# Another order of steps in a kernel of beacon attention and a multiplicative feed-forward layer

## The chip, the cores and the metric

The kernel runs on one core of a Trainium2 chip. The metric is the device time of one launch in microseconds (us), the median of three runs. The profile is of one execution; its span begins with the first instruction of the program, and all times of day in the text are microseconds from that start. TensorE is called PE in the profile, VectorE DVE, ScalarE ACT, GpSimd POOL and SyncE SP.

## The reference

Eight batches with eight heads of 576 positions and 64 elements go through causal attention, in which 16 beacon keys and values stand ahead of the sequence and are seen by all. The result, 4608 tokens of 512 elements, goes through a feed-forward layer that multiplies two projections.

```python
B, H, S, Nb, D = (8, 8, 576, 16, 64)
k_all = np.concatenate([beacon_k, k], axis=2)
v_all = np.concatenate([beacon_v, v], axis=2)
scores = scale * np.matmul(q, k_all.transpose(0, 1, 3, 2))
causal[:, Nb:] = np.triu(np.ones((S, S), dtype=bool), k=1)
scores = np.where(causal, -1000000000.0, scores)
scores = scores - scores.max(-1, keepdims=True)
a = np.exp(scores)
a /= a.sum(-1, keepdims=True) + 1e-09
attn = np.matmul(a, v_all)
# ... transposed to x: (4608, 512)
a = x @ w1            # (512, 1024)
b = x @ w2            # (512, 1024)
h = a * b @ w3        # (1024, 1024)
out = h @ w_out       # (1024, 512)
```

Inputs and output are float32. The kernel computes in float16 with float32 sums.

## The kernel before

The kernel is a set of small steps and a list, `ORDER`, that names them one after another. The list is the program: it is walked once, and each step adds its instructions to the queues of the engines that it uses, in that order. Within an engine the order is kept; between engines semaphores hold back whatever needs something that is not done. The last number of many steps is a bank of PSUM, a letter A or D says whether ScalarE or VectorE copies, and P or S whether GpSimd or SyncE issues a store.

```python
ORDER = """
consts 0; consts 1; consts 2; spin 8 7; lq 0 0 S; lkb 0; lk 0 1 S; lk 0 0 S; lq 0 1 S; lvb 0; lo 0;
lo 1; cast 0 0 q; castb A; l3 0; tq 0 0 6; tn 0 7; cast 0 1 k; l3 1; eq 0 0 A 6; en 0 D 7; l3 2;
tk 0 1 5; cast 0 0 k; l3 5; ek 0 1 A 5; spin 1 7; tk 0 0 6; lo 2; ek 0 0 A 6; lo 3; spin 3 7;
s 0 0 0; s 0 1 2; s 0 2 4; exp 0 0 0; cast 0 1 q; spin 1 7; tq 0 1 6; exp 0 1 2; m 0 0 0; l3 3;
eq 0 1 D 6; exp 0 2 4; m 0 0 1; spin 3 7; s 0 3 0; s 0 4 2; lv 0 1; exp 0 3 0; spin 1 7; s 0 5 4;
# ... 117 lines ...
o 8 0 7; eo 8 1 A 6; st 8 1 S; eo 8 0 A 7; st 8 0 S; o 8 3 6 0 256; eo 8 3 A 6 0 256;
st 8 3 S 0 256; o 8 3 5 256 256; eo 8 3 A 5 256 256; st 8 3 S 256 256
"""
```

The product of w3 and w_out is formed once, as `Wt`, so that a token needs one matrix in place of two. For that each block `r` of w3 (128 rows) is loaded and cast (`l3`), transposed by TensorE (`t3`), copied to SBUF (`e3`) and multiplied with w_out (`f`, four parts; part `a` needs quarter `lo a`), and the result is copied (`ew`). Transposed blocks lie in four places of `gTs[1]`, and block `HELD` in the first 128 columns of the last four store buffers `st8`.

```python
    HELD = 2
    # ...
    def wT(r):

        if r == HELD:
            rows = st8[:, ds(4, 4), 0:P].bitcast(FP16)
        else:
            rows = gTs[1][:, ds(2 * slot["wT", r], 2), :].rearrange("p a (b n) -> p (a b) n", b=2)
        return rows.rearrange("p a (r c) -> p a r c", c=P)

    def l3(r):
        nc.gpsimd.dma_start(w316[:, r // 2, r % 2], moe_w3[ts(r, P), :])

    def lo(a):
        nc.gpsimd.dma_start(wo16[:, ds(2 * a, 2), :], wo_v[a])

    def t3(r, n):
        pt = bank16(n).rearrange("p (r c) -> p r c", c=P)
        for rt in range(NFT):
            nc.tensor.transpose(pt[:, rt, :], w316[:, r // 2, r % 2, ts(rt, P)], ident)

    def f(r, a, n):
        for rt in (2 * a, 2 * a + 1):
            nc.tensor.matmul(
                bank(n),
                wT(r)[:, a, rt % 2, :],
                wo16[:, rt, :],
                start=(rt == 0),
                stop=(rt == NFT - 1),
            )
```

For batch 0, q and k of a pair of heads come in whole through SyncE, in float32, into the buffers `st8` (eight places, in the order of loading; a load into one of the last four waits until `f HELD` has read its part there). VectorE casts them (`cast`) and TensorE transposes them (`tq`, `tk`), ScalarE or VectorE copy them to `qTs` and `kTs` (`eq`, `ek`). For later batches GpSimd's queue loads and casts rows of all heads, and they are transposed either by TensorE (`tq`, `tk`) or by a transfer on SyncE (`Dq`, `Dk`).

```python
    def lq(b, c, e, src=q, z="q"):
        if b == 0:
            nc.sync.dma_start(
                sts[take("own", (z, c), NOWN)][:NR].rearrange("p (h n) -> p h n", h=2),
                src[b, ds(2 * c, 2)].rearrange("h (p j) d -> p h (j d)", j=RUN),
            )
        elif z == "q":
            load_rows(b, c, q, by_heads(q16s[b % NB2]))
        else:
            load_keys(b, c, k, by_heads(k16s[b % NB2]))

    def cast(b, t, z):
        o16 = o16s[z][take("o16" + z, t, 2)]
        nc.vector.tensor_copy(
            o16[:NR].rearrange("p j (h d) -> p h j d", h=2),
            sts[slot["own", (z, t)]][:NR].rearrange("p (h j d) -> p h j d", h=2, j=RUN),
        )

    def tq(b, c, n, z="q"):
        if b == 0:
            o16 = o16s[z][slot["o16" + z, c]]
            for j in range(RUN):
                nc.tensor.transpose(
                    bank16(n)[:, ds(j * NR, NR)], o16[:NR, j, :], ident[:NR, :NR]
                )
            return
        w = rows_of(z, c)
        for t in range(NT):
            nc.tensor.transpose(
                bank16(n)[:, ds(t * P, w)],
                (q16s, k16s)[z == "k"][b % NB2][:w, c, ts(t, P)],
                ident[:w, :w],
            )

    def Dq(b, c):
        rows = rows_of("q", c)
        nc.sync.dma_start_transpose(
            qTs[b % NB2][:, :, ds(c * P, rows)], q16s[b % NB2][:rows, c, :]
        )
```

Scores come in 13 groups for each batch (`s b g bank`), each is exponentiated (`exp`), masked on the diagonal (`m`), multiplied with v (`v`) and divided by its sum (`n`), and the result is transposed by TensorE (`x`, `ex`) or by a transfer (`TX`). The feed-forward layer runs on 512 tokens at a time: `a` and `b` are the two projections, `ea` copies the first, `eb` multiplies, `o` is the product with `Wt`, `eo` the copy and `st` the store.

```python
    def a(mc, kf, n, i=0):
        for kt in range(NKT):
            nc.tensor.matmul(
                bank(n),
                w12[:, kt, ds(i * DF + kf * P, P)],
                xT[:, kt, ds(mc * 512, 512)],
                start=(kt == 0),
                stop=(kt == NKT - 1),
            )

    def o(mc, mt, n, c0=0, w=DM):
        for kf in range(NFT):
            nc.tensor.matmul(
                bank(n)[:, 0:w],
                gTs[mc % 2][:, kf, ts(mt, P)],
                Wt[:, kf, ds(c0, w)],
                start=(kf == 0),
                stop=(kf == NFT - 1),
            )

    def spin(reps, n):
        for _ in range(reps):
            nc.tensor.matmul(bank(n), zeros[:, 0:P], zeros)

    def consts(part):
        if part == 0:
            nc.vector.memset(zeros, 0.0)
            nc.vector.memset(ident, 1.0)
            nc.vector.memset(MX, 1.0)
            nc.vector.memset(MD, 1.0)
            for i in range(NB2):
                nc.vector.memset(kTs[i][:, :, ds(S + Nb, NJT * P - S - Nb)], 0.0)
            nc.vector.memset(ring[:, :, :, GW:GP], 0.0)
            for i in range(NB2):
                nc.vector.memset(vas[i][64:128, 4, :, :], 0.0)
                nc.vector.memset(vas[i][:, 0:4, :, D : D + 1], 1.0)
                nc.vector.memset(vas[i][0 : S + Nb - 4 * P, 4, :, D : D + 1], 1.0)
        elif part == 1:
            nc.gpsimd.affine_select(
                ident,
                ident,
                pattern=[[1, P]],
                compare_op=ALU.is_equal,
                fill=0.0,
                base=0,
                channel_multiplier=-1,
            )
        elif part == 2:
            for msk, base in ((MX[:, 0:112], Nb), (MX[:, 112:192], 0), (MD, 0)):
                nc.gpsimd.affine_select(
                    msk,
                    msk,
                    pattern=[[1, msk.shape[1]]],
                    compare_op=ALU.is_ge,
                    fill=0.0,
                    base=base,
                    channel_multiplier=-1,
                )
```

`spin` multiplies zeros and its result isn't used: it keeps TensorE busy while it has nothing else to do. `consts 1` and `consts 2` make the identity and the two masks; they run on GpSimd, the engine that also issues the casting transfers.

Of the kernel before, what the change touches and what calls it, by code (L numbers as in the profile page):

```python
# [74 lines left out]
f 4 1 5; lq 1 1 P; tq 0 3 6; f 4 2 5; exp 0 7 2; eq 0 3 D 6; v 0 0 1 7; l2 1; m 0 2 0; v 0 0 0 6;
n 0 0 1 7; v 0 2 0 4; s 0 8 0; s 0 9 2; l1 0; n 0 2 0 4; exp 0 8 0; v 0 1 1 7; n 0 0 0 6; f 4 3 5;
lq 1 4 P; n 0 1 1 7; exp 0 9 2; t3 6 6; lk 1 1 P; tk 1 4 4; ew 4 D 5; s 0 10 0; e3 6 A 6;
v 0 1 0 7; ek 1 4 D 4; s 0 11 2; s 0 12 4; lkb 1; n 0 1 0 7; exp 0 10 0; f 6 0 6; m 0 2 1; l2 2;
tq 1 0 7; f 6 1 6; m 0 3 0; exp 0 11 2; eq 1 0 D 7; f 6 2 6; v 0 2 1 7; lv 1 3; exp 0 12 4;
m 0 3 1; t3 7 3; n 0 2 1 7; lq 1 2 P; v 0 3 0 2; e3 7 A 3; v 0 3 1 5; n 0 3 0 2; tq 1 1 7; f 6 3 6;  # L80
l1 2; n 0 3 1 5; eq 1 1 A 7; x 0 0 4; x 0 4 3; ew 6 A 6; f 7 0 2; ex 0 0 D 4; x 0 2 7; ex 0 4 D 3;
x 0 1 6; lq 1 3 P; ex 0 2 A 7; x 0 3 5; ex 0 1 D 6; tq 1 4 4; f 7 1 2; ex 0 3 A 5; eq 1 4 D 4;
lk 1 0 P; f 7 2 2; tk 1 1 6; a 0 1 7; l2 0; ek 1 1 A 6; l1 3; f 7 3 2; ea 0 1 A 7; b 0 4 6;
ew 7 D 2; lk 1 2 P; a 0 0 7; lk 1 3 P; tq 1 2 5; ea 0 0 A 7; b 0 2 4; lk 2 0 P; eq 1 2 D 5;
a 0 2 7; lv 1 2; a 0 4 5; lv 1 0; ea 0 2 A 7; eb 0 2 4; tq 1 3 7; lv 1 1; tk 1 0 3; eq 1 3 A 7;
a 0 5 2; ek 1 0 D 3; b 0 0 7; lk 2 2 P; b 0 1 4; eb 0 0 7; lvb 1; a 0 6 3; eb 0 1 4; lq 2 2 P;
tk 1 2 7; ea 0 4 A 5; ea 0 5 D 2; a 0 3 4; lkb 2; ek 1 2 A 7; ea 0 6 D 3; tk 1 3 5; lq 2 3 P;
b 0 5 7; eb 0 4 6; ek 1 3 A 5; ea 0 3 D 4; lk 2 1 P; s 1 0 0; s 1 1 2; s 1 2 4; eb 0 5 7;
# [593 lines left out]
```

## Time and profile before

| | |
|---|---|
| time, median of three runs | 296.28 us (295.73 to 296.83) |
| span of the profiled execution | 295.1 us |
| busy: TensorE, ScalarE, VectorE, GpSimd | 286.5, 162.8, 156.1, 133.1 us |
| first scores of batch 0 (L492) start | 10.0 us |
| first transposes of w3 (L468) start | 15.2 us |
| bytes moved by the casting queue (GpSimd) and by the plain queue (SyncE) | 26.86 MB and 12.25 MB |

A page of the profile has busy shares, a picture of the span in 40 slices of 7.4 us with a digit for tenths of busy time, the chain of work that ended last (followed back from the end, at each step to what released it), groups of instructions by line of the kernel, and transfers. A line such as `PE one L564 x48` means 48 matmuls of line 564 into a PSUM tile named `one`. Busy times of matmuls overlap each other, since the next starts before the one before it has drained. In a list of waits the columns are: engine and what waited, what it waited for, microseconds in all, how often, and the longest. In a timeline they are the start, the length, the engine, the line and the operation. L345 are the plain loads of q and k of batch 0, L387 those of w_out, L384 of w3, L468 the transposes of w3, L477 the product with w_out, L406 the transposes of q and k of batch 0, L492 scores, L605 warm-up.

### The profile page before, as it was taken

What the parts mean: (1) busy time and instruction counts of PE and PEld (TensorE: products, weight loads), DVE (VectorE), ACT (ScalarE), POOL (GpSimd) and SP (SyncE); (2) the same over time, 40 slices, a digit from 0 to 9 for tenths busy, and PEclk for the clock granted to TensorE, in tenths of its full rate; (3) what the DMA queues carried; (4) which work ended last, traced back from release to release, by engine and by line L of the source; (5) the groups of instructions that cost most, each with busy time, mean ns of one, the idle gap of its engine ahead of it and who ended that gap; (6) DMA issues with size and microseconds to landing.
All of it is one profiled execution on the core that took longest, in us unless ns stands there. A gap on an engine that the chain in (4) does not pass through costs nothing.

```text
span 295.1 us, 7052 instructions
## 1 busy us (share of the span) xinstructions
PE 286.5 (97%) x2914; PEld 156.9 (53%) x2914; DVE 156.1 (53%) x350; ACT 162.8 (55%) x211; POOL 133.1 (45%) x185
## 2 busy tenths in 40 slices
PE   6997999999999999999999999999999999999995
PEld 2454675466665655655545554555456444544443
DVE  5323772786677756765427565466667262430430
ACT  3654794488784975748337542763377233443232
POOL 8464787979866384682288710662001000201000
PEclk9999999999999999999999999999999999999999
DMA  7999999999999999999999992899933110331004
GB/s 169 209 190 252 188 173 171 141 143 129 174 166 144 166 140 187 118 132 155 180 204 162 150 252 25 92 132 168 117 87 97 27 38 0 115 83 71 36 32 149
DMA packets 153617, 39.56 MB, mean 134 GB/s; under 512 B 143217, under 2 KB 150129, under 8 KB 153585
## 3 DMA queue, kind: packets, MB, share of 16 engines
q0 software_dynamic: 114320, 26.86, 99.6%
q1 hardware_dynamic: 39264, 12.25, 28.5%
q8 instruction: 23, 0.38, 0.5%
q14 instruction: 10, 0.07, 0.1%
HBM read 39.32 MB, written 9.44 MB: 165 GB/s over the span
## 4 chain that ended last, share of the span: by engine, by line
PE 83%; DMA 11%; ACT 2%; DVE 1%; issue 1%; POOL 1%; SPq 0%; DVEq 0%; POOLq 0%
PE one L564 38%; PE one L585 20%; PE one L523 9%; PE pair L492 8%; DMA k<-in_k_dram 4%; DMA st<-in_k_dram 4%; DMA kT<-k 3%; PE one L477 3%; ACT ring L502 2%; PE one L605 2%; PE one L412 1%; PE one L549 1%; PE one L468 1%; PE one L406 1%; DVE o16k L394 0%
## 5 line engine op out<-in xcount | busy, mean ns | idle before, releaser
L564 PE MATMUL one<-xT,w 128*128 128x512 f16 x576 | 133.2, 379 | 0.0
L502 ACT ACTIVATE ring<-pair 128x1024 f16<-128x1024 f32 x104 | 99.0, 1027 | 16.0 <-PE pair L492 15.6
L564 PEld LDWEIGHTS <-w 128*128 128x128 f16 x576 | 53.4, 98 | 59.8 <-issue 1.7
L579 DVE TENSOR_TENSOR gT<-one,asb 128x512 f16<-128x512 f32 x72 | 49.1, 689 | 56.9 <-PE one L564 32.9
L585 PE MATMUL one<-Wt,gT 128*128 128x512 f16 (+1 forms) x296 | 66.8, 373 | 0.0
L300 ACT ACTIVATE asb<-one 128x512 f32<-128x512 f32 x52 | 31.0, 597 | 64.9 <-PE one L564 34.1
L599 POOL DMA_DIRECT2D out_dram<-st x32 | 18.1, 565 | 94.3 <-ACT st L300 59.7
L334 POOL DMA_DIRECT2D va<-in_v_dram x40 | 34.0, 857 | 35.4 <-PE one L523 29.9
L585 PEld LDWEIGHTS <-gT 128*128 128x128 f16 x296 | 27.6, 98 | 30.2 <-issue 0.8
L523 PEld LDWEIGHTS <-ring 128*128 128x128 f16 x960 | 34.7, 98 | 9.4 <-issue 1.2
L523 PE MATMUL one<-va,ring 128*128 128x65 f16 x960 | 37.6, 193 | 0.0
L326 POOL DMA_DIRECT2D q<-in_q_dram x35 | 29.9, 856 | 6.2 <-PE one L412 1.7
L535 DVE TENSOR_TENSOR x<-one,rd 128x256 f16<-128x256 f32 (+1 forms) x64 | 31.4, 491 | 2.2
L492 PE MATMUL pair<-qT,kT 64*128 64x80 f16 (+4 forms) x736 | 31.2, 228 | 0.6 <-DMA kT<-k 0.4
L334 POOL DMA_DIRECT2D k<-in_k_dram x35 | 29.7, 854 | 3.3 <-DMA va<-in_v_dram 1.6
L300 ACT ACTIVATE st<-one 128x512 f32<-128x512 f32 (+1 forms) x24 | 13.9, 579 | 31.2 <-PE one L585 31.2
L492 PEld LDWEIGHTS <-kT 64*128 64x128 f16 x736 | 20.7, 96 | 14.1 <-issue 9.1
L512 DVE TENSOR_TENSOR ring<-ring,MD 128x768 f16<-128x768 f16 x32 | 17.7, 552 | 11.4 <-ACT ring L502 11.4
L302 DVE TENSOR_SCALAR asb<-one 128x512 f32<-128x512 f32 x20 | 13.6, 688 | 8.8 <-PE one L564 8.7
L534 DVE RECIPROCAL rd<-one 128x4 f32<-128x4 f32 (+1 forms) x64 | 11.8, 184 | 10.8 <-PE one L523 10.3
L512 DVE TENSOR_TENSOR ring<-ring,MX 128x384 f16<-128x384 f16 x32 | 11.3, 352 | 9.3 <-ACT ring L502 9.3
L477 PE MATMUL one<-wo,gT 128*128 128x512 f16 x56 | 14.8, 380 | 0.4 <-DVE gT L296 0.4
(56 smaller groups left out, 132.5 us busy)
## 6 DMA issues: line engine op xcount, KB each, us to landing
out_dram<-st POOLq DMA_DIRECT2D x32, 256.0 KB, 5.6
q<-in_q_dram POOLq DMA_DIRECT2D x28, 128.0 KB, 6.6
va<-in_v_dram POOLq DMA_DIRECT2D x24, 128.0 KB, 7.6
k<-in_k_dram POOLq DMA_DIRECT2D x21, 128.0 KB, 7.0
xT<-in_moe_w_dram POOLq DMA_DIRECT2D x8, 256.0 KB, 9.8
w<-in_moe_w_dram POOLq DMA_DIRECT2D x8, 256.0 KB, 7.6
st<-in_q_dram SPq DMA_DIRECT2D x4, 288.0 KB, 7.1
st<-in_k_dram SPq DMA_DIRECT2D x4, 288.0 KB, 5.7
```

Of the source, the lines that this page charges most:

```text
L300: nc.scalar.activation(dst, src, AF.Copy, scale=by)
L326: nc.gpsimd.dma_start(dst[:rows, c], src[b, :, ds(c * P, rows), :].rearrange("h s d -> s h d"))
L334: nc.gpsimd.dma_start(dst[ds(p0, rows), c], src[b, :, ds(s0, rows), :].rearrange("h s d -> s h d"))
L477: nc.tensor.matmul(bank(n), wT(r)[:, a, rt % 2, :], wo16[:, rt, :], start=(rt == 0), stop=(rt == NFT - 1),)
L492: nc.tensor.matmul(shape(n, "pair")[:, hh, ds(col, w)], kT[ds(hh * 64, 64), t, ts(jt, P)], qT[ds(hh * 64, 64), t, ds(q0, w)],)
L502: nc.scalar.activation(held(b, g)[:, :, 0:GW], shape(n, "pair"), AF.Exp, scale=scale)
L512: nc.vector.tensor_tensor(blk, blk, msk, ALU.mult)
L523: nc.tensor.matmul(pv[:, 2 * at + hh, 0 : D + 1], held(b, g)[:, hh, ds(col, P)], va[:, jt, 2 * t + hh, 0 : D + 1], start=(jt == 0), stop=( ...
L535: nc.vector.tensor_tensor(x16s[b % NB2][:, ds(2 * h, ni), ts(t, P)].rearrange("p i (h d) -> p i h d", h=2), pv[:, 0 : 2 * ni, 0:D].rearran ...
L564: nc.tensor.matmul(bank(n), w12[:, kt, ds(i * DF + kf * P, P)], xT[:, kt, ds(mc * 512, 512)], start=(kt == 0), stop=(kt == NKT - 1),)
L579: nc.vector.tensor_tensor(gTs[mc % 2][:, kf, :], bank(n), asb[slot["asb", (mc, kf)]], ALU.mult)
L585: nc.tensor.matmul(bank(n)[:, 0:w], gTs[mc % 2][:, kf, ts(mt, P)], Wt[:, kf, ds(c0, w)], start=(kf == 0), stop=(kf == NFT - 1),)
```

## The change

Only `ORDER` changes. All steps, buffers and sizes stay as they are. The list was computed anew, so nearly every line differs; what differs in kind is this:

- GpSimd issues the first quarter of w_out (`lo 0`) ahead of the identity, and the masks (`consts 2`) only behind three quarters of w_out and four blocks of w3. Before, all constants stood first.
- The first loads on SyncE are k, q of the second pair, beacon k, q, k of the second pair; before they were q, beacon k, k of the second pair, k, q of the second pair.
- Blocks 0, 2, 1 and 3 of w3 come first, before 0, 1, 2 and 5. Block 2 is the one held in the store buffers in both. Block 0 is transposed behind three groups of scores, before behind six.
- The last four loads of q and k of batch 0 are q, q, k, k; before k, k, q, q.
- There are 16 warm-up matmuls in five places; before 22 in nine.
- The tile with the last output is the third of its 512 tokens; before the fourth. It is computed in two halves in both.
- One tile of q more is transposed by TensorE (15 in place of 14), and 24 transfers `Dq` are left of 25. Of `x` and `TX`, `Dk` and `tk` the numbers stay, with other tiles.
- VectorE copies six of the eight transposed blocks of w3, before three; ScalarE 57 of the 72 first projections, before 52.

It is meant to have the weights at hand sooner, so that TensorE finds work on `Wt` while the second pair of heads is still on its way, with fewer warm-ups.

```diff
 ORDER = """
-consts 0; consts 1; consts 2; spin 8 7; lq 0 0 S; lkb 0; lk 0 1 S; lk 0 0 S; lq 0 1 S; lvb 0; lo 0;
-lo 1; cast 0 0 q; castb A; l3 0; tq 0 0 6; tn 0 7; cast 0 1 k; l3 1; eq 0 0 A 6; en 0 D 7; l3 2;
-tk 0 1 5; cast 0 0 k; l3 5; ek 0 1 A 5; spin 1 7; tk 0 0 6; lo 2; ek 0 0 A 6; lo 3; spin 3 7;
-s 0 0 0; s 0 1 2; s 0 2 4; exp 0 0 0; cast 0 1 q; spin 1 7; tq 0 1 6; exp 0 1 2; m 0 0 0; l3 3;
-eq 0 1 D 6; exp 0 2 4; m 0 0 1; spin 3 7; s 0 3 0; s 0 4 2; lv 0 1; exp 0 3 0; spin 1 7; s 0 5 4;
-spin 2 7; t3 0 6; l3 4; exp 0 5 4; m 0 1 0; e3 0 D 6; exp 0 4 2; spin 2 7; t3 1 7; lv 0 4; m 0 1 1;
-f 0 0 6; e3 1 D 7; f 0 1 6; lv 0 0; t3 2 5; f 1 0 7; e3 2 A 5; f 1 1 7; lv 0 3; t3 5 4; f 2 0 5;
-e3 5 A 4; f 2 1 5; lk 0 2 S; lv 0 2; f 2 2 5; lk 0 3 S; f 5 0 4; lq 0 2 S; f 1 2 7; f 2 3 5; l1 1;
-f 0 2 6; ew 2 A 5; lq 0 3 S; f 0 3 6; f 5 1 4; ew 0 A 6; l3 6; t3 3 5; f 5 2 4; e3 3 A 5;
-cast 0 2 k; f 5 3 4; f 1 3 7; lk 1 4 P; ew 5 D 4; tk 0 2 6; ew 1 A 7; f 3 0 5; ek 0 2 D 6; f 3 1 5;
-f 3 2 5; cast 0 3 k; f 3 3 5; tk 0 3 6; l2 3; ew 3 A 5; cast 0 2 q; t3 4 7; ek 0 3 A 6; tq 0 2 4;
-e3 4 D 7; lq 1 0 P; eq 0 2 A 4; spin 1 5; f 4 0 5; cast 0 3 q; s 0 6 0; s 0 7 2; l3 7; exp 0 6 0;
-f 4 1 5; lq 1 1 P; tq 0 3 6; f 4 2 5; exp 0 7 2; eq 0 3 D 6; v 0 0 1 7; l2 1; m 0 2 0; v 0 0 0 6;
# ... 106 lines ...
-a 8 5 4; eb 8 3 5; b 8 6 3; ea 8 5 A 4; eb 8 5 6; a 8 6 5; b 8 7 6; a 8 4 4; eb 8 7 6; a 8 0 2;
-ea 8 6 A 5; ea 8 4 D 4; b 8 4 6; eb 8 6 3; ea 8 0 A 2; eb 8 0 7; b 8 1 5; eb 8 4 6; a 8 1 7;
-o 7 1 6; ea 8 1 A 7; eb 8 1 5; o 8 2 7; eo 7 1 A 6; st 7 1 P; o 8 1 6; eo 8 2 A 7; st 8 2 S;
-o 8 0 7; eo 8 1 A 6; st 8 1 S; eo 8 0 A 7; st 8 0 S; o 8 3 6 0 256; eo 8 3 A 6 0 256;
-st 8 3 S 0 256; o 8 3 5 256 256; eo 8 3 A 5 256 256; st 8 3 S 256 256
+consts 0; lk 0 0 S; lq 0 1 S; lo 0; consts 1; spin 8 7; lkb 0; lo 1; lq 0 0 S; lk 0 1 S; l3 0;
+l3 2; l3 1; cast 0 0 k; l3 3; tk 0 0 6; lo 3; consts 2; cast 0 1 q; ek 0 0 A 6; lo 2; castb D;
+spin 2 7; tq 0 1 7; tn 0 6; eq 0 1 A 7; en 0 D 6; cast 0 0 q; l3 4; tq 0 0 5; eq 0 0 A 5;
+cast 0 1 k; spin 3 7; s 0 0 0; s 0 1 2; s 0 2 4; exp 0 0 0; lv 0 2; tk 0 1 6; ek 0 1 D 6;
+exp 0 1 2; spin 2 7; t3 0 7; l3 5; m 0 0 0; s 0 3 0; s 0 4 2; e3 0 D 7; exp 0 2 4; t3 2 6; lv 0 1;
+m 0 0 1; f 0 0 7; exp 0 3 0; e3 2 D 6; f 0 1 7; lvb 0; t3 1 5; exp 0 4 2; m 0 1 0; f 2 0 6;
+e3 1 D 5; f 2 1 6; lq 0 3 S; lv 0 4; s 0 5 0; lq 0 2 S; t3 3 5; exp 0 5 0; f 1 0 4; e3 3 D 5;
+lv 0 0; f 1 1 4; m 0 1 1; f 3 0 3; f 3 1 3; spin 1 5; f 0 2 7; lv 0 3; f 2 2 6; f 2 3 6;
+cast 0 3 q; lk 0 2 S; f 3 2 3; ew 2 A 6; lk 0 3 S; f 3 3 3; f 1 2 4; ew 3 A 3; lq 1 3 P;
+cast 0 2 q; t3 4 6; f 1 3 4; e3 4 A 6; l3 7; tq 0 2 5; ew 1 D 4; tq 0 3 3; f 0 3 7; eq 0 2 A 5;
+eq 0 3 D 3; f 4 0 6; ew 0 A 7; f 4 1 6; cast 0 2 k; f 4 2 6; l1 0; tk 0 2 7; t3 5 5; ek 0 2 A 7;
+f 4 3 6; e3 5 D 5; lk 1 2 P; s 0 6 0; s 0 7 2; ew 4 A 6; cast 0 3 k; f 5 0 7; exp 0 7 2; lkb 1;
+f 5 1 7; l3 6; tk 0 3 6; exp 0 6 0; f 5 2 7; l2 3; ek 0 3 D 6; f 5 3 7; v 0 0 0 5; l1 3; m 0 2 0;
# ... 105 lines ...
+a 8 0 4; ea 8 3 A 6; eb 8 3 7; b 8 7 6; ea 8 0 A 4; eb 8 0 5; b 7 3 7; eb 8 7 6; b 7 6 5; b 7 0 6;
+a 7 3 4; a 7 6 2; ea 7 3 A 4; eb 7 3 7; a 8 5 4; ea 7 6 A 2; eb 7 6 5; a 7 0 7; ea 8 5 A 4;
+eb 8 5 3; o 8 3 5; ea 7 0 A 7; eb 7 0 6; o 7 3 6; eo 8 3 A 5; st 8 3 S; o 7 0 7; eo 7 3 A 6;
+st 7 3 P; o 8 1 6; eo 7 0 A 7; st 7 0 P; o 8 0 7; eo 8 1 A 6; st 8 1 S; o 7 2 6; eo 8 0 A 7;
+st 8 0 S; o 7 1 7; eo 7 2 A 6; st 7 2 P; eo 7 1 A 7; st 7 1 S; o 8 2 6 0 256; eo 8 2 A 6 0 256;
+st 8 2 S 0 256; o 8 2 5 256 256; eo 8 2 A 5 256 256; st 8 2 S 256 256
 """
```

## The prediction

> **What bounds the kernel now.** I read the page first: its share of busy time, its slices, and the chain that ended last; then the chain in order of time, the list of waits for TensorE, and the timelines of the two engines that issue transfers.
>
> ```profile
> PE 286.5 (97%) x2914; PEld 156.9 (53%) x2914; DVE 156.1 (53%) x350; ACT 162.8 (55%) x211; POOL 133.1 (45%) x185
> ...
> PE   6997999999999999999999999999999999999995
> ...
> DMA  7999999999999999999999992899933110331004
> ```
>
> TensorE is busy in 97% of the span and the next engine in 55%. Only slices 1, 4 and the last are thin (a slice is 7.4 us). DMA is full until slice 24 of 40, so TensorE can't run far ahead of the loads either.
>
> ```profile
> 1.75 4.58 DMA st<-in_k_dram
> ...
> 8.77 1.28 PE one L605 x3
> ...
> 19.89 6.25 DMA st<-in_k_dram
> ...
> 173.59 10.36 PE one L564 x48
> ...
> 193.10 11.56 DMA k<-in_k_dram
> 204.68 9.85 DMA kT<-k
> 214.82 1.83 PE one L585 x8
> ...
> 283.42 8.67 PE one L585 x48
> ```
>
> This is the chain (start, length, what). In the middle, 48 matmuls of 512 columns take 10.36 us, 0.216 us each, with nothing between them. At 8.77 us three warm-up matmuls of the same size take 1.28 us, 0.427 each: TensorE is at half speed there. So time is lost in the first 30 us and in the tail, while the middle is matmuls at their rate. What TensorE waited for says the same:
>
> ```profile
> PE one L406 <- DVE o16k L394: 3.2, 2, 1.9
> PE one L605 <- DVE zeros L609: 1.3, 1, 1.3
> PE pair L492 <- DMA kT<-k: 0.4, 2, 0.3
> PE one L477 <- DVE gT L296: 0.4, 1, 0.4
> ```
>
> Only 5.3 us of waiting are named in 295. The largest, 3.2 us, are the casts of k of the first batch, which wait for their loads. These two timelines show how the loads start:
>
> ```profile
> 0.81 0.40 SPq L345 DMA_DIRECT2D st<-in_q_dram  x1
> 1.27 0.43 SPq L359 DMA_DIRECT2D bst<-in_beacon_k_dram  x1
> 1.75 0.92 SPq L345 DMA_DIRECT2D st<-in_k_dram  x2
> 2.71 0.45 SPq L345 DMA_DIRECT2D st<-in_q_dram  x1
> 19.89 0.81 SPq L345 DMA_DIRECT2D st<-in_k_dram  x2
> ```
>
> ```profile
> 2.35 0.71 POOL L370 DMA_DIRECT2D va<-in_beacon_v_dram  x1
> 3.06 1.46 POOL L387 DMA_DIRECT2D wo<-in_moe_w_out_dram  x2
> 4.48 2.19 POOL L384 DMA_DIRECT2D xT<-in_moe_w_dram  x4
> ```
>
> The first four loads of q and k go out on SyncE from 0.81 us. GpSimd, whose queue casts the weights, starts at 2.35 us, behind its constants. The packet records show the plain queue alone until about 4.5 us at 230 GB/s, and the first weight packets only at 6.7 us, when that queue has nearly drained.
>
> **What the Trainium skill says.** "Perfetto Trace Analysis", section "Identifying the Most-Contended Engine", warns that busy time of matmuls does not measure distance from the limit. The trace agrees: a matmul of 512 columns is listed with 379 ns on the page, but they start 0.216 us apart. I therefore count starts, not busy time. "TensorE: Matmul & The Clock Gate", section "Part 1: The HAM clock gate (the "warmup" mystery)", says that the clock is halved until TensorE has been busy through one window of about 3.4 us, and that the window runs freely. The trace agrees on the two rates (0.427 and 0.216 us); the full rate is there from 13.3 us. "DMA: Bandwidth & Descriptors", section "Issuing engines are not separate DMA queues", says that transfers issued by any engine run on the same 16 DMA engines and interleave. From 24 to 28 us the trace agrees: about 65 packets of each queue in each half microsecond. At 4.5 to 6.5 us it agrees less: the later starter got about half as many packets as the other.
>
> **The change part by part.** Only the list of steps changes; all loop bodies, buffers and the arithmetic stay.
>
> Work removed from TensorE: the warm-up matmuls go from 22 to 16 (8+1+3+1+3+1+2+2+1 before, 8+2+3+2+1 after). At 0.216 us that is 6 x 0.216 = 1.3 us; at half speed up to twice that. Transposes: 14 tiles of q go through TensorE before and 15 after, which adds 4 x 0.056 = 0.2 us (eight of L468 take 0.45 us in the chain). Net -1.1 us. The matmuls of the projections, scores and values keep their number, and the last tile of the output is in halves in both lists. Adding every step at its measured spacing gives 271.1 us before and 270.1 after.
>
> Work that moves: I added up this work ahead of the same step in both lists, and compared it with the times in the trace. The seventh group of scores of the first batch stands behind 19.8 us of work and starts at 31.1, so 11.3 us have been lost by then. The first scores of the second batch stand behind 44.6 and start at 56.8 (12.2 lost), of the eighth behind 194.8 at 213.7 (18.9 lost); all of it is 271.1, done at 292 (20.8 lost). From the second batch on the loss grows evenly, about 0.09 us with each of the 91 remaining groups of scores, 8.2 of 8.6 us. It comes with the groups, and stays. What the change can move is the 12 us at the front, small stalls later, and the 3 us tail.
>
> The front, after the change: GpSimd issues the first half-megabyte of w_out at about 0.9 us instead of 3.06, and k, q, beacon k, q, k follow on SyncE. The first packets of that queue came 2.2 us after its first issue (2.35 to 4.5), so now they should come at 3.1 us, when about 190 of the 768 packets of q and k have gone. If the two queues share packet for packet, at about 170 packets a microsecond together, the third big load (q of the first heads, which the first scores need) lands at 8.6 us and the fourth at 10.9, against 7.5 and 8.7 before. Then cast 0.7, six transposes 0.65, copy 0.65 and the warm-up: first scores at 11.2 us, 1.2 later than the 9.98 of before. If the plain queue keeps its precedence, as it had at 4.5 to 6.5 us, they start at about 9.7.
>
> What is gained back: the first block of w3 is transposed right behind three groups of scores and one tile of k, not behind six groups and two warm-ups. Its data are there at about 12.1 us in both. So the transposes start at 12.6 to 14.0 us instead of 15.18. All w3 work moves about 1 to 2 us ahead, and with it the point at which the four loads of the second heads may overwrite the held block. Before, those were issued at 19.89 us, and TensorE stood still for 1.9 us at 24.9 for the first of them. After, the two q go first, at about 17, and k at about 20; I expect a stall of about 1 us at the transposes of q. Loss at the seventh group of scores: 10 to 11 us instead of 11.3.
>
> Later: each load's end in the queue of before (by adding up packets), laid under the new order, shows less room. The tightest load stands 6.7 us of work behind its use for batch 2 in the old order and 7.9 in the new; for the batch 3 tile now transposed by TensorE it is 8.9. With 1.2 us for completion, the new order needs a front loss of at least 10 us to run without waits. So whatever the front gains beyond 1 to 2 us, these waits take back. For batch 8 the same two links of the chain (11.56 and 9.85 us) remain: SyncE issues 12 transposes one behind another, 1.2 to 2 us apart, between the last scores of batch 6 and the first of batch 8; the room is 26.8 us of work against 28.4 before, but one transpose fewer. I count a wait of 0 to 1 us there, as now (0.8).
>
> Sum: -1.1 (work), +1.2 to -1 (front, mid +0.1), +0.7 (less room in the middle, an allowance and not a count), tail 0. Together -0.3 us: 296.28 becomes 296.0.
>
> **The rivals.** First, the early weights crowd out q and k. For it: packets alternate at 24 to 28 us. Against: at 4.5 to 6.5 us the first queue kept its rate. If it is worse than one to one, the first scores come at 12 to 13 us, TensorE has gaps in the window in which it should warm up, and half speed lasts one window (3.4 us) longer, which costs 1.7 us more: 298 to 300.
>
> Second, the transfers become the bound in the middle. For it: DMA is full through slice 24 and the room shrinks by 1 to 3 us for batches 2 to 4; an order made from estimated durations can be wrong in 90 places. Against: the old order comes from the same kind of estimate and shows only 0.8 us of waits behind 31 us. This would make it 297 to 299.
>
> Third, the front gains fully: transposes of w3 at 12.6, no stall for the second heads, and the middle has more room than I count. For it: 2.3 us of the old waits lie exactly there. Then it loses 9.5 us at the front, and the time is 293.5 to 294.5.
>
> **Range and chances.** The work is fixed to 1 us, and the tail is the same; only about 12 us at the front and a few small stalls can move. I take 296.0 us, from 293.4 (third rival) to 299.5 (first) as the range. Two per cent are 5.9 us, half of all that the front loses, so faster by that much has 3%, slower 5% (both bad rivals at once), within 92%.
>
> **What would show it.** In the changed profile: 16 matmuls of L605; the first w_out issue at about 0.9 us and its packets near 3.1; the first scores (L492) at 9.7 to 11.2; the first transposes of L468 at 12.6 to 14.0; waits of L406 for the casts of about 1 us at 23 to 27; the seventh group of scores near 28 to 29; the eighth batch's at 208 to 210 with a wait for kT of at most 1 us; the last matmul near 291. It is wrong if the clock warms up at a different time by a whole window, or if waits for loads of more than 2 us appear between 40 and 110 us.

## The result, and the profile after

| | before | after |
|---|---|---|
| time, median | 296.04 us (295.73 to 296.83, four runs) | 299.19 us (298.85 to 300.02, four runs) |
| ratio to before, 95% interval | 1 | 1.0106 (1.0076 to 1.0137) |
| span of the profiled execution | 295.1 us | 297.3 us |
| first scores of batch 0 | 10.0 us | 12.4 us |
| first transposes of w3 | 15.2 us | 15.0 us |
| first product with w_out (L477) | 16.6 us | 16.6 us |
| seventh group of scores of batch 0 | 31.1 us | 32.5 us |
| first scores of the second batch | 56.8 us | 57.1 us |
| last matmul starts | 291.8 us | 294.0 us |

The change makes the kernel 3.15 us slower, 1.1%. That is less than the 2% that counts as slower here, and inside the predicted range, but I had predicted a gain of 0.3 us. The page after, with the rows of busy shares, TensorE's slices and its granted clock:

```profile
PE 286.3 (96%) x2912; PEld 154.8 (52%) x2912; DVE 153.9 (52%) x348; ACT 163.0 (55%) x214; POOL 133.2 (45%) x184
...
PE   6697999999999999999999999999999999999995
...
PEclk9599899999999999999999999999999999999999
```

TensorE's row differs from that of before in one digit only, 6 in place of 9 in the second slice: in slices of 7.4 us three microseconds are hard to see. The clock row shows half speed in the same slice and a dip in the fifth. A table of windows (length, then the busy time of PE, PEld, DVE, ACT and POOL with the number of instructions, granted clock, DMA share and GB/s) places the loss. First before, then after:

```profile
0.00:30.00 30.00, 25.47 (x200) 13.07 (x200) 11.73 (x31) 15.26 (x19) 17.32 (x31) 1.00 1.23 205
```

```profile
0.00:30.00 30.00, 22.61 (x178) 11.16 (x178) 12.43 (x33) 12.43 (x15) 18.53 (x32) 0.86 1.26 203
```

In the first 30 us TensorE is busy 2.9 us less, with 22 matmul instructions fewer, and its mean granted clock is 0.86. (The clock of before is shown as 1.00 there, but its records begin at 13.3 us, and the warm-up at 8.8 ran at half speed, so the two figures can't be compared.) The list of what TensorE waited for, after:

```profile
PE one L406 <- DVE o16q L394: 3.4, 2, 1.8
PE one L442 <- DVE b L296: 2.8, 1, 2.8
PE one L605 <- DVE zeros L609: 1.3, 1, 1.3
PE one L406 <- DVE o16k L394: 0.3, 1, 0.3
```

A new wait is on the list: 2.8 us for `b`, the cast beacon keys. The named waits grow from 5.3 us (all rows of before) to 7.8. The timeline of the front says when these loads arrive (in brackets: the idle time before the instruction, and what ended it):

```profile
1.34 0.83 POOL L387 DMA_DIRECT2D wo<-in_moe_w_out_dram  x1 [0.82 <-POOLq L666]
8.26 0.41 DVE L296 CAST b<-bst 16x512 f16<-16x512 f32 x1 [2.79 <-DMA bst<-in_beacon_k_dram]
9.91 0.56 DVE L394 CAST o16q<-st 96x768 f16<-96x768 f32 x1 [0.61 <-DMA st<-in_q_dram]
12.10 0.56 DVE L394 CAST o16k<-st 96x768 f16<-96x768 f32 x1 [1.63 <-DMA st<-in_k_dram]
12.40 1.46 PE L492 MATMUL pair<-qT,kT 64*128 64x112 f16 x22
```

The beacon keys, 32 KB, are issued third on SyncE and are cast only at 8.26 us. The q of the first pair of heads is cast at 9.91 and the last of the four large loads at 12.10. The same lines before:

```profile
4.04 0.86 DVE L394 CAST o16q<-st 96x768 f16<-96x768 f32 x1 [0.35 <-DMA st<-in_q_dram]
6.36 0.69 DVE L394 CAST o16k<-st 96x768 f16<-96x768 f32 x1 [1.46 <-DMA st<-in_k_dram]
7.49 0.56 DVE L394 CAST o16k<-st 96x768 f16<-96x768 f32 x1 [0.35 <-DMA st<-in_k_dram]
8.68 0.58 DVE L394 CAST o16q<-st 96x768 f16<-96x768 f32 x1 [0.64 <-DMA st<-in_q_dram]
9.98 1.46 PE L492 MATMUL pair<-qT,kT 64*128 64x112 f16 x22
```

The last of the four casts comes 3.4 us later than before, the first scores 2.4.

Later in the front stands the second loss, the loads of the second pair of heads:

```profile
22.73 0.81 SPq L345 DMA_DIRECT2D st<-in_k_dram  x2
25.15 0.56 DVE L394 CAST o16q<-st 96x768 f16<-96x768 f32 x1 [4.16 <-DMA st<-in_q_dram]
26.52 0.56 DVE L394 CAST o16q<-st 96x768 f16<-96x768 f32 x1 [0.82 <-DMA st<-in_q_dram]
27.14 0.68 PE L406 MATMUL one<-ident,o16q 96*128 96x96 f16 x12 [1.83 <-DVE o16q L394]
```

TensorE stands still for 1.83 us before 27.14. In this execution the granted clock then falls to half from 28.6 to 32.0 us.

The ledger of the prediction (matmul work ahead of a step, warm-up included, set against the time of that step) gives the loss up to it:

| step | lost before | lost after |
|---|---|---|
| seventh group of scores, batch 0 | 31.1 - 19.8 = 11.3 us | 32.5 - 18.1 = 14.4 us |
| first scores, second batch | 56.8 - 44.6 = 12.2 | 57.1 - 41.6 = 15.5 |
| first scores, eighth batch | 213.7 - 194.8 = 18.9 | 212.5 - 189.6 = 22.9 |
| last matmul | 291.8 - 271.1 = 20.7 | 294.0 - 270.1 = 23.9 |

The new order has lost 3.1 us more by the seventh group of scores and 3.2 at the end (4.0 at the first scores of the eighth batch, in between). The difference at the end is there after the first 32 us.

### The profile page after: what moved, and what is told of

Its sections match the earlier page's. It is cut to its first block, busy times and chain, and to the rows that moved or that the text cites. A ratio compares the mean times of both kernels' runs of the same rounds, so it can differ in the third digit from the quotient of the medians.

```text
span 297.3 us, 7051 instructions
## 1 busy us (share of the span) xinstructions
PE 286.3 (96%) x2912; PEld 154.8 (52%) x2912; DVE 153.9 (52%) x348; ACT 163.0 (55%) x214; POOL 133.2 (45%) x184
## 4 chain that ended last, share of the span: by engine, by line
PE 92%; DMA 5%; ACT 1%; DVE 1%; SPq 0%; issue 0%
PE one L564 42%; PE one L585 21%; PE one L523 10%; PE pair L492 9%; PE one L477 3%; DMA st<-in_q_dram 3%; DMA st<-in_k_dram 2%; PE one L412 1%; PE one L468 1%; PE one L549 1%; PE one L605 1%; PE one L406 1%; ACT ring L502 1%; ACT st L300 0%; SPq L345 0%
## 5 line engine op out<-in xcount | busy, mean ns | idle before, releaser
L502 ACT ACTIVATE ring<-pair 128x1024 f16<-128x1024 f32 x104 | 99.5, 1027 | 15.2 <-PE pair L492 15.0
L564 PEld LDWEIGHTS <-w 128*128 128x128 f16 x576 | 52.8, 98 | 59.1 <-issue 3.1
L300 ACT ACTIVATE asb<-one 128x512 f32<-128x512 f32 x57 | 34.1, 598 | 61.3 <-PE one L564 54.7
L334 POOL DMA_DIRECT2D va<-in_v_dram x40 | 34.4, 870 | 24.0 <-PE one L523 18.5
L334 POOL DMA_DIRECT2D k<-in_k_dram x35 | 30.5, 879 | 3.5 <-DMA w<-in_moe_w_dram 1.9
L326 POOL DMA_DIRECT2D q<-in_q_dram x35 | 30.5, 877 | 2.9 <-DMA w<-in_moe_w_dram 0.8
L492 PE MATMUL pair<-qT,kT 64*128 64x80 f16 (+4 forms) x736 | 31.1, 228 | 0.2
L492 PEld LDWEIGHTS <-kT 64*128 64x128 f16 x736 | 19.9, 96 | 16.1 <-issue 12.9
L534 DVE RECIPROCAL rd<-one 128x4 f32<-128x4 f32 (+1 forms) x64 | 11.7, 183 | 12.4 <-PE one L523 12.1
L302 DVE TENSOR_SCALAR st<-one 128x512 f32<-128x512 f32 x13 | 9.0, 691 | 13.8 <-PE one L585 13.8
L477 PE MATMUL one<-wo,gT 128*128 128x512 f16 x56 | 15.2, 397 | 0.0
L512 DVE TENSOR_TENSOR ring<-ring,MX 128x384 f16<-128x384 f16 x32 | 11.3, 352 | 7.5 <-ACT ring L502 7.5
## 6 DMA issues: line engine op xcount, KB each, us to landing
xT<-in_moe_w_dram POOLq DMA_DIRECT2D x8, 256.0 KB, 10.1
```

Of the source, the lines that this page charges most:

```text
L300: nc.scalar.activation(dst, src, AF.Copy, scale=by)
L326: nc.gpsimd.dma_start(dst[:rows, c], src[b, :, ds(c * P, rows), :].rearrange("h s d -> s h d"))
L334: nc.gpsimd.dma_start(dst[ds(p0, rows), c], src[b, :, ds(s0, rows), :].rearrange("h s d -> s h d"))
L477: nc.tensor.matmul(bank(n), wT(r)[:, a, rt % 2, :], wo16[:, rt, :], start=(rt == 0), stop=(rt == NFT - 1),)
L492: nc.tensor.matmul(shape(n, "pair")[:, hh, ds(col, w)], kT[ds(hh * 64, 64), t, ts(jt, P)], qT[ds(hh * 64, 64), t, ds(q0, w)],)
L502: nc.scalar.activation(held(b, g)[:, :, 0:GW], shape(n, "pair"), AF.Exp, scale=scale)
```

## The experiments

The theory, after reading the two traces: with `lo 0` ahead of GpSimd's constants, weight packets are on the DMA engines while q and k are on their way, and the first scores come late. Rivals: TensorE's clock falls back because it idles; it is the place of the beacon load on SyncE; it is the second pair's loads and the order of steps around them.

All twelve in one table, each compared with runs of the kernel before on the same chip:

| kernel | order | first weights issued | beacon load | median us | ratio to before (95%) |
|---|---|---|---|---|---|
| a_warm | new, nine more warm-ups | 1.34 us | third | 298.62 | 1.0037 (1.0013 to 1.0061) |
| a_beacon | new | 1.34 | first | 297.24 | 0.9999 (0.9977 to 1.0022) |
| a_consts | new, constants first | 2.35 | third | 295.38 | 0.9954 (0.9929 to 0.998) |
| b_early | old, `lo 0` early | 1.34 | second | 299.45 | 1.0078 (1.0028 to 1.0127) |
| after_again | new, unchanged | 1.34 | third | 298.58 | 1.0076 (1.005 to 1.0101) |
| a_fill | new, steps moved | 1.34 | third | 299.77 | 1.0109 (1.0071 to 1.0147) |
| a_second | new, loads moved | 1.34 | third | 299.39 | 1.008 (1.0041 to 1.0119) |
| c_fill | a_consts and a_fill | 2.35 | third | 296.47 | 0.9987 (0.9965 to 1.001) |
| c_beacon | new, constants first | 2.35 | first | 296.25 | 0.9997 (0.9977 to 1.0017) |
| a_ident | new, identity first | 1.67 | third | 297.57 | 1.0017 (0.9995 to 1.004) |
| b_third | old | 3.06 | third | 295.44 | 0.9953 (0.9927 to 0.9978) |
| a_fourth | new | 1.34 | fourth | 298.72 | 1.0055 (1.0033 to 1.0076) |

**a_warm: keep TensorE busy in the wait for the second pair.**

```diff
-... e3 4 A 6; l3 7; tq 0 2 5; ew 1 D 4; ...
+... e3 4 A 6; l3 7; spin 9 5; tq 0 2 5; ew 1 D 4; ...
```

> The changed kernel with nine warm-up matmuls (9 x 0.216 = 1.9 us) in front of the transposes of q of the third pair, where TensorE waits from 25.1 to 27.1 us. If the clock is the cause (in the profile of the changed kernel it is at half speed from 28.8 to 32.2 us, behind this wait), the half-speed stretch goes and the time falls by up to 1.7 us against the changed kernel, to about 297.5. If the early casting queue or the order in the middle is the cause, nothing is gained, and the added matmuls cost 0 to 0.5 us: 299.2 to 299.7.

298.62 us, against 299.19 and 298.58 for the new order itself. In its profile the clock stays at full speed from 15.7 us on, so the fall at 28.6 is gone, but the last matmul starts at 293.7 instead of 294.0. By ratio it lies 0.4 to 0.7% below the two measurements of the new order, by median 0 to 0.6 us; the intervals overlap with those of the repeat. So this fall of the clock costs nothing by median, and half of the loss or somewhat more by ratio; the runs don't say which. It isn't the whole loss, since a_warm is still 0.4% slower than before by ratio. The run shows one thing more: nine matmuls of 0.216 us are 1.9 us of added work and made the kernel no slower; they lie in a wait.

**a_consts: the identity and both masks ahead of the weights again, nothing else.**

```diff
-consts 0; lk 0 0 S; lq 0 1 S; lo 0; consts 1; spin 8 7; ...
+consts 0; lk 0 0 S; lq 0 1 S; consts 1; consts 2; lo 0; spin 8 7; ...
-... lo 3; consts 2; cast 0 1 q; ...
+... lo 3; cast 0 1 q; ...
```

> The changed kernel with all constants ahead of the first load of w_out on GpSimd, as in the kernel before. If the early casting queue costs the difference, this gives back 1 to 2 us (297.2 to 298.2) and the first scores start at 10.5 to 11.5 us. If the clock or the beacon load costs it, less than 0.7 us is given back.

295.38 us: 1.2 to 1.5% below the new order, and below the kernel before. The same timeline lines of this kernel:

```profile
2.35 1.63 POOL L387 DMA_DIRECT2D wo<-in_moe_w_out_dram  x2
7.02 0.71 DVE L394 CAST o16q<-st 96x768 f16<-96x768 f32 x1
8.60 0.56 DVE L394 CAST o16k<-st 96x768 f16<-96x768 f32 x1 [0.87 <-DMA st<-in_k_dram]
9.14 1.46 PE L492 MATMUL pair<-qT,kT 64*128 64x112 f16 x22
```

One microsecond later for the weights is 2.9 us earlier for the first q (7.02 against 9.91) and 3.3 us earlier for the first scores. The wait for `b` is not on its list. Its ledger has lost 29.3 - 18.1 = 11.2 us at the seventh group of scores and 290.8 - 270.1 = 20.7 at the end, both as before. The windows of the DMA traffic in the decisive two microseconds, first the new order, then this kernel (the last number is GB/s):

```profile
4.00:5.00 1.00, 1.00 (x10) 0.35 (x8) 0.64 (x2) 0.00 (x0) 1.00 (x2) 1.00 1.11 140
5.00:6.00 1.00, 0.96 (x11) 0.33 (x7) 0.47 (x1) 0.64 (x2) 1.00 (x2) 1.00 0.97 186
```

```profile
4.00:5.00 1.00, 1.00 (x6) 0.21 (x5) 0.56 (x1) 0.00 (x0) 1.00 (x2) 1.00 1.15 238
5.00:6.00 1.00, 0.72 (x8) 0.23 (x5) 0.56 (x2) 0.64 (x1) 1.00 (x2) 1.00 1.09 247
```

With the early weights the sixteen DMA engines are as busy (1.11 and 0.97 against 1.15 and 1.09) and are listed with a third fewer bytes. But that third is a matter of counting. The list of transfers of before has beacon k of one batch, always the same amount, in two lines, first through the casting queue, then through the plain one (size, and the time from issue to landing):

```profile
k<-in_beacon_k_dram POOLq DMA_DIRECT2D x7, 16.0 KB, 4.6
bst<-in_beacon_k_dram SPq DMA_DIRECT2D x1, 32.0 KB, 3.0
```

A casting transfer is listed with its size in float16, half of the float32 that it reads; so are its packets (1024 of 1024 bytes for the whole of w_out, 1.05 MB, where its float32 is 2.10 MB). The packet records of the two microseconds have 196 weight packets of 1024 bytes, 65 large packets of q and k (1536 bytes) and 99 small beacon packets in the new order; in a_consts they have 34, 273 and 118. With the weights counted as float32 this is 0.53 MB against 0.52: no less traffic, but other traffic. The early weights took the place of q and k.

**b_early: the one early load alone, in the old order.**

```diff
-consts 0; consts 1; consts 2; spin 8 7; ... lvb 0; lo 0;
+consts 0; lo 0; consts 1; consts 2; spin 8 7; ... lvb 0;
```

> The kernel before with the first quarter of w_out ahead of the constants on GpSimd, and nothing else changed. If the early casting queue alone costs the difference, this is 1.5 to 3 us slower than the kernel before (297.5 to 299). If it takes the beacon load behind two big loads, or the clock, to make the loss, it stays within 0.7 us of 296.0, since the beacon load is second here and gone before the casting queue starts.

299.45 us, 0.8% slower than before. The casts of k move from 6.4 and 7.5 us to 8.0 and 10.1, and the first scores from 10.0 to 12.6:

```profile
7.99 0.56 DVE L394 CAST o16k<-st 96x768 f16<-96x768 f32 x1 [3.46 <-DMA st<-in_k_dram]
10.08 0.56 DVE L394 CAST o16k<-st 96x768 f16<-96x768 f32 x1 [1.44 <-DMA st<-in_k_dram]
12.57 1.46 PE L492 MATMUL pair<-qT,kT 64*128 64x112 f16 x22
```

The later identity is not the reason: the first transposes, which need it, start at 4.60 us, before at 4.96. With a_consts this settles the main point from both sides: with the constants ahead of the weights the new order wins back more than the change lost, and the early load alone, put into the old order, costs 2.5 us at the median of this batch (before: 296.98). What stays open is the window from 3 to 4 us, where b_early moved 159 GB/s against 221 before, with only one packet of the casting queue in it.

**a_ident: only the identity ahead of the weights, a smaller dose.**

```diff
-consts 0; lk 0 0 S; lq 0 1 S; lo 0; consts 1; spin 8 7; ...
+consts 0; lk 0 0 S; lq 0 1 S; consts 1; lo 0; spin 8 7; ...
```

> The new order with only the identity ahead of the first quarter of w_out; the masks stay behind the weights. The first weights go out some 0.3 to 0.6 us later than in the new order and some 0.5 us earlier than with both constants first. If the loss grows evenly with how early the weights start, about half comes back: 297 us, first scores at about 11. If what counts is that the beacon load's small packets are through before the first weight packets, nearly all comes back: 295.5 us, first scores at 9.1 to 9.6. If the order of GpSimd's constants is not the cause, it stays at 298.6.

297.57 us, about half of the way. Weights issued at 1.34, 1.67 and 2.35 us give the q of the first pair cast at 9.9, 8.3 and 7.0, first scores at 12.4, 10.0 and 9.1, and medians near 298.6 to 299.2, 297.6 and 295.4. The loss grows with how early the weights start; at the front most of it comes with the last third of a microsecond. The masks stay behind the weights here and the first scores still come at 10.0, so late masks are not what holds them up.

**The place of the beacon load: a_beacon, c_beacon, b_third, a_fourth.** It is 128 packets of 256 bytes, where a large load is 192 packets of 1536. First a_beacon, the new order with this load in front:

```diff
-consts 0; lk 0 0 S; lq 0 1 S; lo 0; consts 1; spin 8 7; lkb 0; lo 1; ...
+consts 0; lkb 0; lk 0 0 S; lq 0 1 S; lo 0; consts 1; spin 8 7; lo 1; ...
```

> The changed kernel with the load of beacon k first on SyncE in place of third. If the small packets of this load (256 bytes, 4.4 to 7.6 us) hold back the q and k behind them, q and k of the first pair land 2 us earlier and the first scores start at about 10.5 us in place of 12.4. If what is lost lies at the front, the time falls by 1 to 2 us, to 297.2 to 298.2; if the first w3 blocks and not q and k bound the front, the scores come earlier but the time stays at 298.5 to 299.5, but for the clock, which may fall differently.

297.24 us, level with before. First scores at 10.4, though the weights start as early as in the new order. At this point the small load looked like the culprit: it stood in the traffic of two queues and held up what came behind. Three runs tested that. c_beacon has it in front and the constants first (the edits of a_consts and a_beacon together):

> The new order with the identity and masks first, and the beacon load first on SyncE as well. If the early weights are the cause, and the place of the beacon load matters only because weight packets come between, the beacon load's place is worth nothing once the weights start late: about 295.4 us, as with the constants alone. If the beacon load's small packets cost by themselves wherever they stand in front of q and k, their move brings another 1 us as it did with early weights: about 294.3. It could also cost up to 0.5 us, since the first k then goes out 0.45 us later.

296.25 us. It is neither as fast as a_consts nor faster: in front, the small load costs 0.4% by ratio when the weights are late (the two intervals just touch). And with the small load in front, early weights cost nothing (a_beacon 0.9999, c_beacon 0.9997), where with the load third they cost 1.2% or more: what early weights cost depends on what stands in the plain queue. b_third moves it, in the old order and with late weights, behind one large load more:

```diff
-... spin 8 7; lq 0 0 S; lkb 0; lk 0 1 S; lk 0 0 S; lq 0 1 S; ...
+... spin 8 7; lq 0 0 S; lk 0 1 S; lkb 0; lk 0 0 S; lq 0 1 S; ...
```

> The old order with the beacon load third on SyncE, behind the first q and k of the second pair, as in the new order, and the constants first as ever. If the beacon load is slow only because weight packets stand beside it, nothing changes: 296 to 297 us, ratio to before within 0.3 per cent of 1. If its place among the loads costs by itself, the last two loads land about 1 us later and it is about 297.5.

I expected no change, or a loss. It gains 0.5% (295.44 us), as much as anything here:

```profile
3.94 0.56 DVE L394 CAST o16q<-st 96x768 f16<-96x768 f32 x1 [0.24 <-DMA st<-in_q_dram]
5.11 0.56 DVE L394 CAST o16k<-st 96x768 f16<-96x768 f32 x1 [0.62 <-DMA st<-in_k_dram]
6.85 0.56 DVE L394 CAST o16k<-st 96x768 f16<-96x768 f32 x1 [0.30 <-DMA st<-in_k_dram]
7.63 0.56 DVE L394 CAST o16q<-st 96x768 f16<-96x768 f32 x1 [0.22 <-DMA st<-in_q_dram]
...
8.65 1.46 PE L492 MATMUL pair<-qT,kT 64*128 64x112 f16 x22
```

Before, the second to fourth of these casts stood at 6.4, 7.5 and 8.7 us: all three are 0.6 to 1.3 us earlier, and the first scores 1.3. So the place of the small load matters by itself, and with late weights third is the better place, not the worse one. Last, a_fourth keeps the early weights and takes the small load out of the way of the first q altogether:

```diff
-... spin 8 7; lkb 0; lo 1; lq 0 0 S; lk 0 1 S; l3 0;
+... spin 8 7; lo 1; lq 0 0 S; lkb 0; lk 0 1 S; l3 0;
-... lo 2; castb D; spin 2 7; tq 0 1 7; tn 0 6; eq 0 1 A 7; en 0 D 6; cast 0 0 q; l3 4; tq 0 0 5; eq 0 0 A 5;
+... lo 2; spin 2 7; tq 0 1 7; eq 0 1 A 7; cast 0 0 q; l3 4; tq 0 0 5; eq 0 0 A 5; castb D; tn 0 6; en 0 D 6;
```

> The new order with its early weights as they are, and the beacon load fourth on SyncE, behind the q of the first pair; its cast and transposes stand behind those of that q. Theory: the loss comes about where the beacon load's 128 small packets meet the weight packets with large loads behind them. Then the q of the first pair no longer waits for them, is cast near 7.5 to 8.5 in place of 9.9, the first scores come at 9.5 to 10.5 in place of 12.4, and the time is 295.5 to 297. Rival: any early weights take half of the plain queue's share, whoever stands in it. Then q gains only the beacon load's own 0.6 us, the first scores stay at 11.8 or later and the time at 298 to 298.6. Third way: q comes early, but the beacon load is now itself the last of what the first scores need, and they come at 11 to 12: 297.5.

298.72 us: the theory that the small load alone holds q up falls, and the rival holds. The first q gains only 0.4 us although nothing small stands in front of it, and the first scores come at 12.5. Its waits and that cast:

```profile
PE one L406 <- DVE o16q L394: 5.6, 2, 3.8
```

```profile
9.54 0.56 DVE L394 CAST o16q<-st 96x768 f16<-96x768 f32 x1 [3.64 <-DMA st<-in_q_dram]
```

The wait that bore the name of `b` in the new order now bears the name of q, and is longer. What stood on the list as a wait for the beacon keys was a wait for the loads that were on their way beside the weights.

One thing stays open: why a_beacon escapes, though its weights are as early. The packet records show that there the first quarter of w_out went through in one go (56, 91 and 80 packets in the three half microseconds from 4.5 us, the plain queue down to 12 in between) and then the plain queue ran nearly alone (110 and 90), at 254, 234 and 330 GB/s in the windows from 4 to 7 us; in the new order the packets of both queues were mixed all the way, at 140, 186 and 219. With casting packets counted as float32 it is 326, 409 and 352 against 239, 288 and 260, so here the traffic did differ. What decides between the two was not tried.

**The second pair of heads: a_second and a_fill, with a repeat of the new order.**

```diff
 a_second
-... lq 0 2 S; t3 3 5; ... lv 0 3; f 2 2 6; f 2 3 6; cast 0 3 q; lk 0 2 S; f 3 2 3; ew 2 A 6; lk 0 3 S; ...
+... lq 0 2 S; f 2 2 6; lk 0 2 S; f 2 3 6; lk 0 3 S; t3 3 5; ... lv 0 3; cast 0 3 q; f 3 2 3; ew 2 A 6; ...
 a_fill
-... l3 7; tq 0 2 5; ew 1 D 4; tq 0 3 3; f 0 3 7; eq 0 2 A 5; eq 0 3 D 3; f 4 0 6; ew 0 A 7; f 4 1 6; cast 0 2 k; f 4 2 6; ...
+... l3 7; ew 1 D 4; f 0 3 7; f 4 0 6; ew 0 A 7; f 4 1 6; f 4 2 6; tq 0 2 5; tq 0 3 3; eq 0 2 A 5; eq 0 3 D 3; cast 0 2 k; ...
```

> The changed kernel unchanged, beside its variants on the same chip. If its time is a matter of the order of the loads, it stays 0.8 to 1.4% above the kernel before. If the difference was luck of the clock's phase, it comes within 0.4%.

> The changed kernel with the last two parts of the held block's product moved ahead of block 3's transposes, so that both loads of k are issued with those of q at about 19 us and not at 22.7. If the late issue of these loads costs the stretch, k lands 2 to 3 us earlier, the stretch falls to 14 to 15 us, and 0.8 to 2 us come back. If q alone bounds it, nothing comes back, since q is issued no earlier and shares the queue with k.

> The changed kernel with four products of w3 and w_out (4 x 0.43 = 1.7 us of work that TensorE has to do anyway) moved ahead of the transposes of q of the third and fourth pair, into the wait at 25 to 27 us. If the wait for the loads of these pairs is what the new order loses behind the front (15.9 us from the first product with w_out to the seventh group of scores, against 14.5 before), 1.2 to 1.7 us come back, more where the clock then stays up. If the loads of k right behind them bound that stretch, the wait only moves and less than 0.5 us comes back.

298.58, 299.39 and 299.77 us: no gain from either. In a_fill four products go ahead of the transposes of q; the wait moves to k:

```profile
PE one L406 <- DVE o16k L394: 2.8, 1, 2.8
PE one L442 <- DVE b L296: 1.6, 1, 1.6
PE one L406 <- DVE o16q L394: 1.6, 1, 1.6
```

In a_second both loads of k go out at 19.8 and 20.5 us instead of 22.7 and 23.2, and the stall before q is 1.9 us, as in the new order (1.8). In its profiled execution, the second fastest of its seven (297.24 us), k is cast at 28.7 in place of 30.0 and the stretch from the first product to the seventh group of scores takes 14.1 us in place of 15.9, as expected; the median shows nothing of it. Both kinds of wait end with the loads, not with TensorE's order. c_fill is a_fill with the constants first:

> The changed kernel with the constants first on GpSimd and with the same four products moved into the wait. If the two losses are separate and add up, this is faster than either edit alone: 1.5 us for the wait and 3 us for the front, 0.99 to 0.993 of the kernel before, which beats both kernels. If they hide each other, it stays at the 0.995 of the constants alone.

296.47 us; over its 22 runs the moved steps add nothing to a_consts (295.38) either. The one execution profiled is the fastest of the 22 (293.57 us): the clock was at full speed from 5.7 us on, without a fall, and the last matmul started at 288.4. That the clock makes it so fast is likely but not shown.

## Why the prediction was right and wrong

The number lay 3.2 us from the result and the sign was wrong. The range held it only because its upper end, 299.5, was set by the first rival ("the early weights crowd out q and k", 298 to 300), and that is what happened. Point by point:

**The front (+1.2 to -1 us): this step failed.** My sum let the two queues share packet for packet: the other 386 of the 576 packets of the first three large loads, at 85 a microsecond from 3.1 us, were through at 7.6, and 1.0 us more for the landing gave 8.6; for the last k 10.9. They landed at 9.9 and 12.1, 1.2 to 1.3 us later each, and the first scores came at 12.4 in place of 9.7 to 11.2, at least 1.2 late as well. The count itself held, at 7.3 us, but by luck: I had left the beacon load's 128 packets out, and the plain queue was faster than I took it to be (all 704 packets by 7.3 us, 122 a microsecond). What failed was the 1.0 us between count and landing: it was 2.6 us in the new order, and in a_consts 1.4 (5.6 to 7.0). A count over all engines hides that some run behind. "DMA: Bandwidth & Descriptors" in the Trainium skill, section "Queues, rings and completion order", would have warned me: a queue has a ring of its own on each engine, and its work is taken in order only within one engine. The traces agree: the plain queue still gives a few packets in each half microsecond from 9.0 us on (13, 11, 7), long after the bulk has gone. Its record also has 80 packets of 4 bytes, which fits one closing mark from each of sixteen engines for each of the five loads; 77 of them had come when the third large load landed, so by this reading 13 of the sixteen parts of the fourth were through while a part of the third was still on its way. The other branch of this step, that the plain queue keeps its precedence, rested on a misreading: what I saw beside it from 4.5 to 6.5 us before was 104 packets of 128 bytes of beacon v and no weights.

**Gained back at w3 (transposes at 12.6 to 14.0, all w3 work 1 to 2 us ahead): failed by the same step.** The transposes came at 15.0, since the scores ahead of them were late, and the first product at 16.6 as before. With the constants first it happened as predicted, and more: transposes at 11.8, first product at 13.4, 3.2 us ahead of before.

**The second pair (a stall of about 1 us, loss of 10 to 11 us at the seventh group of scores): too small a loss.** The loads of q went out at 18.5 and of k at 22.7, not 17 and 20. The stall was 1.8 us and the loss 14.4. Even in a_consts the new order gives its lead back here: 3.2 us ahead at the first product, 1.8 at the seventh group of scores (29.3 against 31.1), of which the smaller work accounts for 1.7.

**Fewer warm-ups (-1.3 us of work) and one transpose of q more (+0.2): right as bookkeeping, not as a gain that can be counted on.** The list is 1.0 us shorter and the loss 3.2 us longer. In a_warm nine warm-ups inside a wait cost nothing that can be seen, so those taken out of waits would save nothing. Whether some of the six removed stood outside waits was not tried apart.

**Less room in the middle (+0.7) and the tail (0).** Right in the middle, and too small to matter. From the first scores of the second batch to those of the eighth the ledger loses 7.4 us after and 6.7 before, the 0.7 allowed for; the tail behind it takes 1.0 us after and 1.8 before. From the seventh group of scores to the end the two are level, 9.5 and 9.4. The second rival, transfers as the bound in the middle, is out.

**The clock.** I named a whole window at half speed, 1.7 us, as part of the first rival. The profiled execution shows half speed from 8.1 to 14.9 us (before, full speed is on record from 13.3, 1.6 us earlier) and again from 28.6 to 32.0. The first fall lies in the wait for `b`, the second comes 1.5 us after the end of a wait. Removing the second alone (a_warm) brought nothing by median and 0.4 to 0.7% by ratio. And a_consts, whose profile has a fall behind the same wait (25.5 to 28.9), is faster than before, so the clock alone doesn't make the difference.

**What the new order is worth.** a_consts and b_third, the two lists each with late weights and the beacon load third, stand at 0.9954 and 0.9953 of before. So the new order gains nothing measurable over the old one that the place of this one load doesn't bring as well. Its reduced work and its 1.7 us lead at the first product (13.4 against 15.1) are gone by the seventh group of scores (29.3 in both); in the profiled execution of a_consts a fall of the clock from 25.5 to 28.9 us, behind the wait for the second pair, is likely to have taken part of it. By median these two are the fastest kernels of the study, 1.6 and 1.5 us under the kernel before at the medians of their batches.

## What to carry to other kernels

Where the first compute step waits for a load, a second queue that starts a microsecond earlier may cost three, as here, where its packets took the place of those that were waited for: put the transfers that nothing needs yet behind those that are needed first, and test it by moving the issue alone. Compare landing times from the trace, not packet counts: here a load landed 1.4 to 2.6 us after the count was reached. Before you compare GB/s, look at whether casting transfers are listed with the size read or written. And when a wait vanishes from the list, look for the same time under another name: here it moved from the beacon keys to q, and from q to k.

## What the runs showed of the hardware

- The profile lists a casting transfer with its float16 size (beacon k of one batch: 16.0 KB through the casting queue, 32.0 KB through the plain one). Before, the casting queue alone is listed with 203 to 216 GB/s from 8 to 11 us, which is 406 to 432 of float32 read; the plain queue alone moved 239 and 221 GB/s from 2 to 4 us.
- Counted so, the new order and a_consts moved the same from 4 to 6 us (0.53 and 0.52 MB), with 65 and 273 large packets of q and k in it. In a_beacon, whose weights are as early as in the new order, it was 0.73 MB; the reason stays open.
- A load of 32 KB in packets of 256 bytes, put second, delayed the large loads behind it by 0.6 to 1.3 us (before against b_third, where it stands third). In front of all, it leaves the windows from 2 to 3 us at 92 and 114 GB/s (a_beacon and c_beacon) where the others have 223 to 255.
- The first packets of the casting queue came 2.5 us after the start of its first issue in the new order (1.34 to 3.83), and 1.9 to 3.2 us after it over all runs (b_third, c_beacon).
- The granted clock can fall after less idling than the Trainium skill suggests. "TensorE: Matmul & The Clock Gate", section "Why this matters for your kernels", warns of gaps of more than about 3 us; here it fell after a wait of 1.83 us with 0.68 us of transposes behind it. The measurement decides. The length of the wait alone doesn't settle it: with waits of 1.62 us (the repeat of the new order), 1.92 (a_second), 2.02 (a_beacon) and 2.24 (c_beacon) in that place the clock stayed at full speed, with 2.06 (a_consts) it fell.
